# VectorE's clamp and shift of the decoded weights, walked in two interleaved halves

## The chip, the cores and the metric

The kernel runs on one core of one Trainium2 chip. The metric is the device time of one execution in microseconds. Three runs of the kernel before took 690.2, 690.53 and 690.93 us, median 690.53 us. All times below are microseconds unless marked ns, counted from the start of the profiled execution's span.

## The reference

Two stages. First an attention for 8 batches of 8 heads, 576 positions and 64 columns a head, through 32 packed queries p: the packed queries attend to k and v, and q attends to the packed result. Then a feed-forward layer on its output, 4608 tokens of 512 columns, hidden width 2048:

```python
def sm_attn(qq, kk, vv):
    s = scale * np.matmul(qq, kk.transpose(0, 1, 3, 2))
    s = s - np.max(s, axis=-1, keepdims=True)
    a = np.exp(s)
    a = a / (np.sum(a, axis=-1, keepdims=True) + 1e-09)
    return np.matmul(a, vv)
p_packed = sm_attn(p, k, v)
out = sm_attn(q, p_packed, p_packed)
...
h = x @ w_in
g = 0.5 * h * (1.0 + erf(h * inv_sqrt2))
return (g @ w_out).astype(np.float32)
```

The weights `w_in` (512 x 2048) and `w_out` (2048 x 512) reach the kernel as float64, 8 bytes an element, that is as two 32-bit words each.

## The kernel before

The work is cut into 16 units: four pairs of batches by four blocks of 512 hidden columns. For each unit TensorE multiplies the packed attention result with its block of `w_in` ("wps", L1582), the second attention's weights with that ("h", L1662 for the first unit, L1671 for the others), ScalarE applies the gelu (L1703), and TensorE multiplies the result with `w_out` ("o", L1733 to L1735, later L1922). The first matrices are split into a high and a low part (VectorE, L1712 for the gelu's result, L1300 and L1598 for others), so that three fast products make one precise one.

The weights are decoded once, in 32 tiles of 128 partitions by 512 elements, within the first 190 us: 8 tiles for each of the four blocks of hidden columns. The decode of one tile (`decode`, from L1427) goes over three engines. A DMA brings the raw words (L1441 or L1445). ScalarE puts the absolute high word into the tile's first half `t` (L1453) and the scaled low word into `full` (L1455; for two tiles of the first block GpSimd does that, L1460). VectorE then works on `t` in three instructions: a clamp of the high word between two limits (L1467), a shift left by three bits with a mask (L1468), both in place and with one tensor as source, and the return of the sign bits from the raw words (L1474), with two tensors as sources. GpSimd adds `full` (L1494 or L1509). For `w_out` there follow the split into two parts (ScalarE L1499, GpSimd L1516) and the differences of blocks (GpSimd L1533) that later units use.

`t` is one half of a slot of a large buffer, `memory`: 512 words of 4 bytes that lie one behind the other in each partition.

The order of every engine's instructions is written out by hand as lists of numbers (`TURNS`), replayed once when the program is built; a cost given to an operation there (0.85 for L1467 and L1468 together) decides nothing but the order in which the engines' streams are written. Each engine takes its instructions strictly in that order and waits by semaphores for the others. Until the first output product TensorE is kept busy by matmuls on zeros (L1640) at places that a table, `WARM`, names.

Two things around the decode matter for the prediction. PSUM has a ring of two buffers, `wide`, which wps and h tiles take in turn; a tile takes its buffer when the copy or the gelu that reads the tile before it in that buffer is over. And in the first unit VectorE does, in its written order between decode steps: the copies of two of the four wps tiles (L1593), transposes (L1220, L1289), maxima and sums of the softmaxes (L1238, L1278 to L1280).

Of the kernel before, what the change touches and what calls it, by code (L numbers as in the profile page):

```python
# [10 lines left out]
F32 = mybir.dt.float32  # L11
# [4 lines left out]
ALU = mybir.AluOpType  # L16
# [23 lines left out]
W_LEAST = 2.0 ** -15  # L40
W_MOST = 122880 - 2.0 ** -7
# [583 lines left out]
def packed_attention_gelu_ffn(ctx: ExitStack, tc: tile.TileContext, q, k, v, p, w_in, w_out, out):  # L625
# [12 lines left out]
    nc = tc.nc  # L638
# [44 lines left out]
    def plan(order):  # L683
# [743 lines left out]
        def decode(u, i, part, load_step, step):  # L1427
            n, f = f"{u}_{i}_{part}", u % NF
# [35 lines left out]
            t, full = both[:, 0], both[:, 1]  # L1464

            def rebias():
                nc.vector.tensor_scalar(t.bitcast(F32), t.bitcast(F32), W_LEAST, W_MOST, ALU.max, ALU.min)  # L1467
                nc.vector.tensor_scalar(t, t, 3, 0x3FFFFFF8, ALU.logical_shift_left, ALU.bitwise_and)  # L1468

            def high_word():  # L1470
                yield Op(DVE, 0.85, step, rebias, port=True, hold=holds[1])
                yield Op(
                    DVE, 0.685, step,
                    lambda: nc.vector.scalar_tensor_tensor(t, high, -0x40000000, t, ALU.bitwise_and, ALU.bitwise_or),  # L1474
                    port=True)
# [753 lines left out]
```

## Time and profile before

| | |
|---|---|
| median of 3 runs | 690.53 us (690.2 to 690.93) |
| the profiled execution | 690.13 us, span 688.3 us |
| granted TensorE clock, mean | 0.998 |
| PE busy | 676.2 us, 98% |
| VectorE busy | 517.7 us, 75% |
| ScalarE busy | 384.2 us, 56% |
| GpSimd busy | 317.4 us, 46% |
| chain that ended last | PE 94%, DMA 3%, ACT 1%, DVE 1% |

The span runs from the first to the last instruction; the execution's own time is 1.8 us longer. PE is TensorE's matmuls, PEld its weight loads, DVE VectorE, ACT ScalarE, POOL GpSimd. A busy PE includes the matmuls on zeros. Shares over the whole span hide that the decode is a matter of the first 190 us alone, so the stretches are looked at one by one. A line of the profile such as L1467 is a line of the kernel.

### The profile page before, as it was taken

To read this page: it belongs to the slowest core of one execution; us is meant where nothing else is said; L and a number is where in the kernel's file an instruction comes from. 1 tells how busy PE (TensorE), PEld (TensorE's weight loads), DVE (VectorE), ACT (ScalarE), POOL (GpSimd) and SP (SyncE) were. 2 spreads that over 40 slices of the span, in tenths; PEclk is the share of its full clock that TensorE was granted. 3 is DMA by queue.
4 is the path that set the end of the run, shared out by engine and by line. 5 is a ranking of instruction groups with operands and counts; after the bars stand their busy time and mean duration, and the time that the engine had idled before them with its cause. 6 is when DMAs were issued, how large, how long until landed. Compare 5 with 4: busy or idle time off the path is not lost.

```text
span 688.3 us, 13110 instructions
## 1 busy us (share of the span) xinstructions
PE 676.2 (98%) x5098; PEld 555.8 (81%) x5098; DVE 517.7 (75%) x719; ACT 384.2 (56%) x602; POOL 317.4 (46%) x298
## 2 busy tenths in 40 slices
PE   8899999999999999999999999999999999999997
PEld 6668787897878897788888897877978898879885
DVE  5898988787887736788888856687888845655785
ACT  5888777766655764464565464464546455443331
POOL 4686784484460835052246733232232653333462
PEclk9999999999999999999999999999999999999999
DMA  9987999988619799999333599999616474543354
GB/s 329 337 197 211 226 253 236 288 301 224 246 55 339 225 216 219 209 214 305 106 118 132 180 232 191 197 238 236 238 62 211 113 243 147 190 123 113 133 183 138
DMA packets 183101, 140.32 MB, mean 204 GB/s; under 512 B 144128, under 2 KB 153856, under 8 KB 183040
## 3 DMA queue, kind: packets, MB, share of 16 engines
q1 hardware_dynamic: 181168, 138.44, 72.3%
q10 hardware_dynamic: 1872, 1.05, 0.6%
q8 instruction: 40, 0.66, 0.4%
q14 instruction: 21, 0.17, 0.1%
HBM read 109.05 MB, written 30.41 MB: 203 GB/s over the span
## 4 chain that ended last, share of the span: by engine, by line
PE 94%; DMA 3%; ACT 1%; DVE 1%; issue 0%; SPq 0%; ACTq 0%
PE o L1922 34%; PE h L1671 27%; PE o L1733 6%; PE o L1735 6%; PE o L1734 6%; PE wps L1582 4%; PE h L1662 2%; DMA wraws<-in_moe_w_out_dram 2%; PE s L982 2%; PE pp L1173 1%; DMA memory<-in_k_dram 1%; PE e1Tm L1086 1%; PE o_edge L1735 1%; PE o_edge L1734 1%; PE o_edge L1733 1%; PE o L1640 0%
## 5 line engine op out<-in xcount | busy, mean ns | idle before, releaser
L1922 PE MATMUL o<-rounded 128*128 128x512 f32 (+1 forms) x1014 | 249.9, 392 | 0.7 <-DVE memory L1967 0.4
L1922 PEld LDWEIGHTS o<-rounded 128*128 128x128 f32 x1014 | 183.9, 188 | 46.7 <-issue 9.1
L1671 PE MATMUL h<-a2T,wp 128*128 128x288 f32 x1440 | 207.1, 295 | 0.7 <-ACT memory L1703 0.7
L1671 PEld LDWEIGHTS h<-a2T,wp 128*128 128x128 f32 x1440 | 200.6, 188 | 8.0 <-ACT memory L1703 1.0
L1783 POOL TENSOR_TENSOR memory<-memory 128x1024 f32<-128x1024 f32 x36 | 89.3, 2482 | 126.9 <-DVE rounded L1873 61.4
L1873 DVE TENSOR_TENSOR rounded<-memory,rounded 128x1024 fp32r<-128x1024 f32 x82 | 109.8, 1345 | 36.5 <-ACT rounded L1867 33.4
L1867 ACT CAST rounded<-memory 128x1024 fp32r<-128x1024 f32 x84 | 88.0, 1052 | 87.8 <-PE o L1922 54.4
L1967 DVE TENSOR_TENSOR memory<-o,memory 128x512 f32<-128x512 f32 x124 | 82.1, 680 | 40.5 <-PE o L1922 40.3
L1696 ACT ACTIVATE memory<-h 128x576 f32<-128x576 f32 x96 | 61.6, 651 | 81.8 <-PE h L1671 78.7
L1796 POOL TENSOR_TENSOR memory<-memory 128x1024 f32<-128x1024 f32 x12 | 30.3, 2526 | 109.0 <-ACT memory L1696 109.0
L1733 PE MATMUL o<-rounded 128*128 128x512 f32 x176 | 71.2, 405 | 0.0
L1735 PE MATMUL o<-rounded 128*128 128x512 f32 x176 | 68.8, 391 | 0.0
L1734 PE MATMUL o<-rounded 128*128 128x512 f32 x176 | 68.7, 390 | 0.0
L1598 DVE TENSOR_TENSOR wp<-wps,wp 128x1024 fp32r<-128x1024 f32 x30 | 36.2, 1219 | 22.8 <-ACT wp L1593 22.7
L1733 PEld LDWEIGHTS o<-rounded 128*128 128x128 f32 x176 | 33.1, 188 | 12.5 <-issue 6.1
L891 DVE STREAM_TRANSPOSE memory<-memory 128x1152 f32<-128x1152 f32 x24 | 32.6, 1367 | 10.9 <-DMA memory<-in_k_dram 8.0
L1509 POOL TENSOR_TENSOR memory<-memory 128x512 int32<-128x512 int32 x16 | 23.5, 1471 | 34.6 <-DVE memory L1474 26.0
L1735 PEld LDWEIGHTS o<-rounded 128*128 128x128 f32 x176 | 33.0, 188 | 7.2
L1734 PEld LDWEIGHTS o<-rounded 128*128 128x128 f32 x176 | 33.1, 188 | 5.2
L1593 ACT CAST wp<-wps 128x1024 fp32r<-128x1024 f32 x30 | 29.7, 1016 | 12.9 <-PE wps L1582 12.9
L1703 ACT ACTIVATE memory<-h 128x576 f32<-128x576 f32 x32 | 20.6, 650 | 23.3 <-PE h L1671 13.8
L1582 PE MATMUL wps<-memory,pp 64*32 64x512 f32 (+1 forms) x544 | 32.8, 571 | 0.0
(160 smaller groups left out, 880.9 us busy)
## 6 DMA issues: line engine op xcount, KB each, us to landing
rounded<-ws SPq DMA_DIRECT2D x48, 512.0 KB, 4.7
rounded<-wx_s SPq DMA_DIRECT2D x36, 512.0 KB, 4.4
memory<-ws SPq DMA_DIRECT2D x24, 512.0 KB, 5.6
wraws<-in_moe_w_out_dram SPq DMA_DIRECT2D x16, 512.0 KB, 5.6
ws<-rounded SPq DMA_DIRECT2D x16, 512.0 KB, 6.1
memory<-in_v_dram SPq DMA_DIRECT2D x15, 512.0 KB, 7.3
memory<-in_k_dram SPq DMA_DIRECT2D x48, 144.0 KB, 6.0
memory<-in_q_dram SPq DMA_DIRECT2D x48, 144.0 KB, 5.2
```

The lines of the kernel that those rows point to most:

```text
L1582: nc.tensor.matmul(t[r0:r0 + 32, hh, :m], lhsT=pp[b][rows, hh, r0:r0 + 32], rhs=wi[u, hh][rows, g, cols], start=True, stop=True)
L1598: yield Op(DVE, 1.22, step, lambda: nc.vector.tensor_tensor(lo, x, hi.bitcast(F32), ALU.subtract))
L1671: nc.tensor.matmul(t[:, half, :HALF], lhsT=w[:, wpart, ch, fc], rhs=a2T[b, ch][:, apart, half * HALF:(half + 1) * HALF], start=ch == 0 and ...
L1696: lambda: nc.scalar.activation(x[:, c % 2].rearrange("p (a n) -> p a n", a=2), t[:, :, :HALF], AF.Gelu), table="gelu")
L1733: nc.tensor.matmul(t, lhsT=g[0], rhs=w[:, 0], start=first, stop=False)
L1734: nc.tensor.matmul(t, lhsT=g[0], rhs=w[:, 1], start=False, stop=False)
L1735: nc.tensor.matmul(t, lhsT=g[1], rhs=w[:, 0], start=False, stop=last)
L1783: return Op(POOL, 2.4, 0, lambda: nc.gpsimd.tensor_tensor(of(x), of(y), of(z), op))
L1867: o = op[u, m] = yield Op(ACT, 1.04, 0, lambda o: nc.scalar.copy(o[:, 0], x), [(ops, f"op_{u}_{m}")])
L1873: engine, cost, 0, lambda: on(engine).tensor_tensor(o[:, 1], x, o[:, 0].bitcast(F32), ALU.subtract), port=True)
L1922: nc.tensor.matmul(t[:, cols], lhsT=x[:, wpart], rhs=o[:, part, q, cols], start=first and q == 0 and wpart == 0 and part == 0, stop=q == 1 ...
L1967: yield Op(DVE, 0.685, 0, lambda: nc.vector.tensor_tensor(to(), x, to(), ALU.add))
```

## The change

`t`, 512 words in a row per partition, is looked at as two halves of 256 words, and the two VectorE instructions walk it with the halves as the inner dimension: word 0, word 256, word 1, word 257, and so on. 256 words of 4 bytes are 1 KB. Both instructions read and write the same words as before, in place, with the same limits, shift and mask; only the order of the words within one instruction differs. In the built program their access goes from one dimension of 512 steps of 1 word to 256 steps of 1 word outside and 2 steps of 256 words inside. L1474, which follows, still walks straight on. No instruction, wait or place in an engine's order changes; the lines below L1466 move down by one.

```diff
             def rebias():
-                nc.vector.tensor_scalar(t.bitcast(F32), t.bitcast(F32), W_LEAST, W_MOST, ALU.max, ALU.min)
-                nc.vector.tensor_scalar(t, t, 3, 0x3FFFFFF8, ALU.logical_shift_left, ALU.bitwise_and)
+                x = t.rearrange("p (a n) -> p n a", a=2)
+                nc.vector.tensor_scalar(x.bitcast(F32), x.bitcast(F32), W_LEAST, W_MOST, ALU.max, ALU.min)
+                nc.vector.tensor_scalar(x, x, 3, 0x3FFFFFF8, ALU.logical_shift_left, ALU.bitwise_and)
```

## Rows read from the trace of the kernel before

**Rows 1.** Busy time by stretch: its bounds, its length, each engine's, clock, DMA.

```profile
0.00:20.00 20.00, 16.23 (x137) 12.32 (x138) 11.54 (x24) 11.23 (x21) 8.22 (x15) 1.00 0.93 339
20.00:60.00 40.00, 38.00 (x484) 26.50 (x483) 37.90 (x72) 34.37 (x68) 31.08 (x27) 1.00 0.85 241
60.00:190.00 130.00, 129.26 (x984) 106.42 (x983) 108.06 (x160) 91.45 (x165) 77.45 (x90) 1.00 0.89 251
190.00:688.30 498.30, 492.70 (x3498) 410.51 (x3497) 360.21 (x466) 247.20 (x350) 200.60 (x166) 1.00 0.68 183
```

**Rows 2.** TensorE's waits, 45 to 200 us: in total, times, longest.

```profile
PE h L1671 <- ACT memory L1703: 0.7, 1, 0.7
```

**Rows 3.** TensorE's waits, 0 to 45 us.

```profile
PE o L1640 <- issue: 1.4, 1, 1.4
```

**Rows 4.** VectorE's timeline, 20 to 52 us: start, duration, line; in brackets idle time before.

```profile
20.79 0.43 DVE L1467 TENSOR_SCALAR memory<-memory 128x512 f32<-128x512 f32 x1 [0.73 <-ACT memory L1453]
21.26 0.71 DVE L1468 TENSOR_SCALAR memory<-memory 128x512 int32<-128x512 int32 x1
...
23.58 0.93 DVE L1467 TENSOR_SCALAR memory<-memory 128x512 f32<-128x512 f32 x1
24.55 0.43 DVE L1468 TENSOR_SCALAR memory<-memory 128x512 int32<-128x512 int32 x1
...
29.64 0.38 DVE L1467 TENSOR_SCALAR memory<-memory 128x512 f32<-128x512 f32 x1
30.06 0.43 DVE L1468 TENSOR_SCALAR memory<-memory 128x512 int32<-128x512 int32 x1
...
33.33 0.70 DVE L1467 TENSOR_SCALAR memory<-memory 128x512 f32<-128x512 f32 x1
34.07 1.26 DVE L1468 TENSOR_SCALAR memory<-memory 128x512 int32<-128x512 int32 x1
...
39.74 0.78 DVE L1289 STREAM_TRANSPOSE memory<-memory 128x576 f32<-128x576 f32 x1 [0.17 <-POOL memory L1283]
40.44 0.79 DVE L1467 TENSOR_SCALAR memory<-memory 128x512 f32<-128x512 f32 x1
41.27 1.38 DVE L1468 TENSOR_SCALAR memory<-memory 128x512 int32<-128x512 int32 x1
...
47.30 1.38 DVE L1467 TENSOR_SCALAR memory<-memory 128x512 f32<-128x512 f32 x1
48.71 0.43 DVE L1468 TENSOR_SCALAR memory<-memory 128x512 int32<-128x512 int32 x1
49.05 0.68 DVE L1593 COPY wp<-wps 128x512 f32<-128x512 f32 x1
```

**Rows 5.** Weight loads of the tile h, 48 to 53 us: ns min/median/max, first and last start.

```profile
L1662 PEld LDWEIGHTS h<-memory,wp x16: 188/190/190, 48.6 to 52.2; 128*128 128x128 f32 x16
```

**Rows 6.** The two changed lines in the whole span, columns as in rows 5.

```profile
L1467 DVE TENSOR_SCALAR memory<-memory x32: 364/430/1376, 7.5 to 188.4; 128x512 f32<-128x512 f32 x32
L1468 DVE TENSOR_SCALAR memory<-memory x32: 426/427/1405, 7.9 to 188.8; 128x512 int32<-128x512 int32 x32
```

**Rows 7.** VectorE's groups by shape, 0 to 200 us: busy us, mean ns, idle before.

```profile
L2127 DVE TENSOR_TENSOR memory<-o,memory 128x512 f32<-128x512 f32 x16 | 10.7, 684 | 3.1 <-PE o L1735 3.1
L1598 DVE TENSOR_TENSOR wp<-wps,wp 128x1024 fp32r<-128x1024 f32 x6 | 7.1, 1218 | 0.3 <-ACT wp L1593 0.2
L1474 DVE SCALAR_TENSOR_TENSOR memory<-wraw,memory 128x512 int32<-128x512 int32 x4 | 2.8, 693 | 0.1
```

**Rows 8.** ScalarE's groups by shape, 0 to 200 us.

```profile
L1059 ACT ACTIVATE memory<-memory,mx 128x576 f32<-128x576 f32 x4 | 3.1, 768 | 0.0
L1059 ACT ACTIVATE memory<-s,mx 128x576 f32<-128x576 f32 x4 | 3.0, 758 | 1.3 <-DVE mx L1051 1.1
```

**Rows 9.** GpSimd's groups by shape, 0 to 200 us.

```profile
L1460 POOL TENSOR_SCALAR memory<-wraw 128x512 int32<-128x512 uint32 x1 | 1.6, 1594 | 0.1
```

**Rows 10.** GpSimd's timeline, 46 to 49 us.

```profile
46.78 1.61 POOL L1263 TENSOR_TENSOR memory<-memory,mx 128x576 f32<-128x576 f32 x1
```

## The prediction

> **What bounds the kernel now.** I read the busy time by stretch first. In each of the three stretches from 20 us on TensorE is busy for at least 95% of the time [rows 1]; from 60 us to the end its idle time is 0.74 + 5.6 us, so what comes late there is little. The granted clock is 1.00 in every stretch. VectorE has the decode in the first 190 us alone: it is busy 37.9 of the 40 us from 20 to 60 us, and only 108.1 of the 130 us after that [rows 1]. TensorE's list of waits agrees. Between 45 and 200 us there is a single wait of 0.7 us, for ScalarE [rows 2]. Before 45 us one of the two longest is 1.4 us of "issue", in which the profile shows nothing that TensorE waited for [rows 3]; most of the others there are for loads. So the end is set by the sum of TensorE's work from about 50 us on, plus the time at which the start-up lets it begin; a change on VectorE costs time only where it makes TensorE stop.
>
> The place where that can be is read in VectorE's timeline from 20 to 52 us [rows 4]. It starts with a wait of 0.73 us for ScalarE (20.79), and from then on VectorE runs nearly back to back: the only wait of any size is 0.17 us for GpSimd (39.74). The run ends, for TensorE, in the copy of wps at 49.05 us (L1593), over at 49.73. That copy frees the PSUM buffer wps_0_1_0, which is one of the two in the ring `wide`; the ring is taken in turn by wps_0_1_0, h_2, h_3, so h_3 needs it. The 16 weight loads of h_2 and h_3 begin between 48.6 and 52.2 us [rows 5]; the ninth, h_3's first, is thus at 48.6 + 8 x 3.6 / 15 = 50.5 us. TensorE has 0.8 us to spare there, of which I count 0.76 and leave the rest for the semaphore.
>
> **The change part by part.** No instruction is added, removed or moved: the two TENSOR_SCALARs of each of 32 decoded tiles keep their 512 elements, their place and their waits. Only their walk differs: columns 0, 256, 1, 257 and so on, read and written. So there is one unknown, the new duration, and one sum.
>
> The duration today: median 430 and 427 ns [rows 6]. An operation of VectorE with two sources takes 693 ns for the same 512 elements (L1474); from 684 ns for 512 elements (L2127) to 1218 ns for 1024 (L1598) it is 534 ns for 512 more, so 1.04 ns each and about 0.15 us fixed [rows 7]. The clamp's 0.43 us less 0.15 is 0.55 ns an element: it handles two at a time. No row shows VectorE walking with a jump at every element, so the cost is bounded from both sides. The low end is nothing: L1474 reads every second word of the raw weights and is no slower than L2127; and ScalarE's exponential takes 758 ns where it reads PSUM in steps of 32 words (L1059, source s), against 768 ns where it reads SBUF straight on [rows 7, 8]. Below nothing I see one way only, the second rival. The high end is the slowest row for these 512 elements on any engine, GpSimd's 1594 ns in L1460 [rows 9], 1.16 us more per instruction. I take 0.69 us, the row of L1474, because it is VectorE's own on the same tile and it is what comes out if the jump takes away the second element of a turn or, equally, if each pair takes two turns (0.15 + 2 x 0.28 = 0.71). So +0.26 us per instruction.
>
> [...]
>
> The sum. Eight instructions lie before 20 us (a count of the timeline), where VectorE is busy 11.5 of 20 us [rows 1] and the run of rows 4 opens with a wait for ScalarE, whose weights a DMA brings; their 8 x 0.26 us fit into such waits, and I count nothing. If that cover were gone, they could add 2.1 us at most. From 20.79 to 48.71 us there are twelve [rows 4]: 12 x 0.26 = 3.12 us, one behind the other, since VectorE has no idle time between them. GpSimd's work in this stretch waits for VectorE and shifts with it, so it hides nothing: the run of L1263 at 46.78 us [rows 10], behind which the clamp at 47.30 takes 1.38 us, is fed by VectorE itself. Less 0.17 us (the wait at 39.74) and less 0.76 us (h_3's room) that is 2.19 us by which h_3 starts later. TensorE has no idle time from there to 179 us to win it back.
>
> After 50 us: the other 44 of the 64 instructions (32 of each line [rows 6], less 8 and 12), the last at 188.8 us, 44 x 0.26 = 11.4 us against 130 - 108.1 = 21.9 us of idle VectorE from 60 to 190 us [rows 1]. TensorE waits for no VectorE result in this stretch [rows 2], so I count nothing; the cover is the idle time, and it is gone at 21.9 / 44 = 0.50 us per instruction at the latest, earlier where the idle time lies in the wrong places. So the profiled execution of 690.13 us (span 688.3, 1.8 outside it) would become 692.3 us; the median of 690.53 us becomes **692.7 us**.
>
> **The rivals.** (A) *The jump is free*, or something on the way to the chip straightens the walk, so that the change does not do what it says: 0.43 us stays, and the time is 690.5 us. For it speak the rows of L1059 and L1474 named above; against it, that neither is a jump on VectorE. [...]
>
> (B) *VectorE drops to one element per turn and thereby stops shutting out GpSimd*, the case that is not slower. The clamps now take up to 1.38 us when they meet GpSimd's work [rows 4, 10], so they wait for one another. With 0.69 us each and no such wait, the twelve of rows 4 take 8.3 us, where they now take 9.25: the run ends 0.95 us earlier. TensorE takes little of it, as h_3 has room already; the most is the 0.7 us wait at 179 us [rows 2]: 689.8 to 690.5 us. Against it: the median of either line is 0.43 us [rows 6], so at least half of these instructions meet nobody, and those get slower. It decides only if the two-element mode is lost. [...]
>
> (C) *The jump costs both*: one element per turn and two turns for each, 0.15 + 2 x 0.53 = 1.2 us, +0.79 us per instruction. Then VectorE itself is the bound: 56 instructions from 20 to 190 us add 44 us against 2.1 + 21.9 = 24 us of idle time, so +20 us at least, and up to 64 x 0.79 = 51; I put it at +27, 717 us. It begins where the idle time no longer suffices: at +0.4 us per instruction I expect +5 to +9 us, since TensorE's waits start before all idle time is used.
>
> **How the numbers follow.** What a measurement of this kernel can tell from no change is about 0.2%, 1.4 us. The forecast, a price of 0.12 to 0.35 us per instruction, has 0.55: 12 x 0.12 - 0.93 = +0.5 us at its low end (691.0) and 12 x 0.35 - 0.93 = +3.3 us at its high end, with another 1 us because the later stretch begins to lose (694.8). Within it, below 0.19 us per instruction, the sum stays under 1.4 us; I give that 0.14. A has 0.24, B 0.05 and C with its first part 0.16. Slower by over 0.2% is 0.41 + 0.16 = 0.57; within 0.2% is 0.14 + 0.24 + 0.02 = 0.40; faster 0.03, the best of B and chance. The range goes from 690.0 us, which holds A, to 700 us, which takes in C's first part; left out are the heavy end of C and the best of B. The likeliest case alone is 691.0 to 694.8 us.
>
> **What would show it.** Rows of L1467 and L1468 with a median near 690 ns, and some still over 1 us beside GpSimd, confirm the price and the mode; a maximum no longer above 0.75 us means B, a median of 430 means A. The copy of wps at 49.05 us should be about 3 us later and h_3's weight load about 2.2 us later, with a wait of TensorE for VectorE there; from 60 to 190 us TensorE should show no new wait for VectorE, and VectorE's busy time from 20 to 60 us should fill the stretch. The prediction is wrong if the duration lies outside 0.55 to 0.78 us, if h_3 starts on time although it is 0.69, or if new waits of TensorE turn up after 60 us.

## The result, and the profile after

The changed kernel takes 697.65 us (median of four runs, 697.08 to 698.24) beside 690.73 us for the kernel before in the same job: ratio 1.0102, 95% interval [1.0084, 1.0121], so 7.0 us slower. (Such ratios here and below compare runs at the usual granted clock; one run further down had an execution of 953 us at a mean clock of 0.655, which its ratio leaves out.) The forecast was 692.7 us in a range of 690.0 to 700 us: the direction and the range hold, but the likeliest case, 691.0 to 694.8 us, does not hold the time. It was +2.2 us and became +7.0 us. The profiled execution of after took 697.08 us (span 695.3), 6.95 us more than that of before.

The page's chain of work that ended last was PE 94%, DVE 1% before; now it is PE 83%, DVE 10%. VectorE has come onto the path. Where, the busy time by stretch tells (bounds, length, then PE, PEld, DVE, ACT, POOL, each with its instructions, clock, DMA):

```profile
0.00:20.00 20.00, 15.50 (x134) 11.28 (x135) 14.11 (x24) 11.33 (x21) 7.21 (x14) 1.00 0.93 341
20.00:60.00 40.00, 36.36 (x475) 24.40 (x474) 38.11 (x67) 31.86 (x63) 30.11 (x24) 1.00 0.83 237
60.00:190.00 130.00, 126.80 (x954) 101.70 (x954) 124.76 (x158) 87.92 (x161) 82.91 (x88) 1.00 0.88 239
```

Against [rows 1] VectorE's busy time rises by 2.6 us in the first stretch and by 16.7 us from 60 to 190 us, where its idle time falls from 21.9 to 5.2 us. TensorE, which had 0.74 us idle there, now has 3.2. The granted clock is 1.00 everywhere, as before.

TensorE's waits from 45 to 200 us (in total, times, longest), where [rows 2] has one row:

```profile
PE o L1736 <- DVE rounded L1713: 1.8, 1, 1.8
PE h L1672 <- ACT memory L1704: 0.7, 1, 0.7
PE e1Tm L1086 <- ACT memory L1704: 0.3, 1, 0.3
PE h L1663 <- DVE wp L1594: 0.3, 1, 0.3
PE h L1672 <- DVE pT L958: 0.2, 1, 0.2
```

Four of the five were not there, three of them for VectorE, and the longest is for L1713, the split of the gelu's result, which was not a changed line at all. Comparing the start of the same matmul in both traces, TensorE is 2.64 us late at h_3 (the place of [rows 5], 50.78 us before), 3.0 at 64, 3.8 at 90, 5.9 at 104 and 6.9 by 200 us; from there the delay stays. So some 2.6 us come from the start-up and 4.3 us from the stretch behind it. Most of the 2.6 us is there long before h_3: TensorE is on time until 26.7 us, then stops at a matmul on zeros and is 2.0 us late behind it. In its waits before 45 us this is now the longest row; L909 is a copy of transposed inputs out of PSUM.

```profile
PE o L1641 <- DVE memory L909: 1.9, 1, 1.9
```

The two changed instructions in the whole span, against [rows 6] (ns min/median/max, first and last start):

```profile
L1468 DVE TENSOR_SCALAR memory<-memory x32: 626/787/1829, 7.3 to 195.2; 128x512 f32<-128x512 f32 x32
```

```profile
L1469 DVE TENSOR_SCALAR memory<-memory x32: 657/730/1778, 8.0 to 195.9; 128x512 int32<-128x512 int32 x32
```

The three instructions of VectorE's part of the decode by shape, 0 to 200 us (busy us, mean ns, idle before), first of before, then of after:

```profile
L1474 DVE SCALAR_TENSOR_TENSOR memory<-wraws,memory 128x512 int32<-128x512 int32 x28 | 20.9, 749 | 0.5
L1468 DVE TENSOR_SCALAR memory<-memory 128x512 int32<-128x512 int32 x32 | 20.0, 624 | 1.1
L1467 DVE TENSOR_SCALAR memory<-memory 128x512 f32<-128x512 f32 x32 | 19.3, 602 | 7.5 <-ACT memory L1453 7.4
```

```profile
L1468 DVE TENSOR_SCALAR memory<-memory 128x512 f32<-128x512 f32 x32 | 31.1, 971 | 1.4 <-ACT memory L1453 1.2
L1469 DVE TENSOR_SCALAR memory<-memory 128x512 int32<-128x512 int32 x32 | 28.3, 884 | 1.1
...
L1475 DVE SCALAR_TENSOR_TENSOR memory<-wraws,memory 128x512 int32<-128x512 int32 x28 | 25.1, 898 | 0.5
```

The mean of the clamp goes from 602 to 971 ns and that of the shift from 624 to 884 ns, 0.31 us more on average. L1475 became slower too, although nothing was done to it: 749 to 898 ns.

VectorE's timeline at the two ends of the stretch of [rows 4], and at the copy that TensorE waits for:

```profile
21.15 0.88 DVE L1468 TENSOR_SCALAR memory<-memory 128x512 f32<-128x512 f32 x1 [0.76 <-ACT memory L1453]
...
26.51 1.48 DVE L1475 SCALAR_TENSOR_TENSOR memory<-wraws,memory 128x512 int32<-128x512 int32 x1
...
28.17 0.54 DVE L909 COPY memory<-o 128x384 f32<-128x384 f32 x1
...
52.69 0.67 DVE L1594 COPY wp<-wps 128x512 f32<-128x512 f32 x1
```

The first row stood at 20.79 us before, so the first eight instructions left only 0.36 us behind. The sign return in the second row took 0.69 us (25.01) and the copy L909 stood at 25.88: it is 2.29 us late. The copy of wps in the last row stood at 49.05: it is 3.64 us late.

### The profile page after: what moved, and what is told of

It is laid out like the page before. It is cut to its first block, busy times and chain, and to the rows that moved or that the text cites. A ratio compares the mean times of both kernels' runs of the same rounds, so it can differ in the third digit from the quotient of the medians.

```text
span 695.3 us, 13110 instructions
## 1 busy us (share of the span) xinstructions
PE 678.1 (98%) x5098; PEld 554.4 (80%) x5098; DVE 542.0 (78%) x719; ACT 384.4 (55%) x602; POOL 324.5 (47%) x298
## 4 chain that ended last, share of the span: by engine, by line
PE 83%; DVE 10%; DMA 3%; issue 1%; SPq 1%; ACT 0%; POOL 0%; DVEq 0%; ACTq 0%; POOLq 0%
PE o L1923 34%; PE h L1672 26%; PE o L1734 5%; PE o L1736 5%; PE o L1735 5%; PE wps L1583 4%; DVE memory L1468 2%; PE s L982 2%; DMA wraws<-in_moe_w_out_dram 1%; DVE memory L1475 1%; DVE rounded L1713 1%; DVE memory L1469 1%; PE pp L1173 1%; DMA memory<-in_k_dram 1%; PE e1Tm L1086 1%
```

## The experiments

Two questions were open: what the price per instruction consists of, and by which way 7 us come of it. The first group of runs asks both: one walks pairs of words, two interleave only a part of the tiles, and one keeps the straight walk but makes VectorE's decode longer. The edits are against the changed kernel.

**Pairs of adjacent words.** Words 0, 1, 256, 257, and so on.

```diff
-                x = t.rearrange("p (a n) -> p n a", a=2)
+                x = t.rearrange("p (a n two) -> p n a two", a=2, two=2)
```

> The two halves are interleaved by pairs of adjacent words (0, 1, 256, 257, 2, 3, ...) instead of word by word, so the 1 KB jumps stay but half as many. Theory J (the price is that every element of a walk lies apart from the one before): both instructions go back to 0.43 us and the kernel to the time of before, 690.5 us (within 1 us). Rival D (any second dimension in the walk, or any 1 KB jump, costs): 0.55 to 0.70 us each, and the kernel at +3 to +7 us.

690.66 us, ratio 1.0003 [0.9993, 1.0013]; the clamp is back at nearly the old price:

```profile
L1468 DVE TENSOR_SCALAR memory<-memory x32: 376/468/1539, 7.5 to 187.6; 128x512 f32<-128x512 f32 x32
```

So a walk between the two halves costs next to nothing as such (38 ns in the median, nothing in the time), and it is not one more dimension that costs; the jump at every single word does.

**Only the first block of hidden columns** (the 8 tiles decoded in the start-up), and **only the other three** (24 tiles):

```diff
+                x = t.rearrange("p (a n) -> p n a", a=2) if u == 0 else t
```

```diff
+                x = t.rearrange("p (a n) -> p n a", a=2) if u > 0 else t
```

> The interleaved walk in the first block of hidden columns alone: 8 of the 32 tiles, 16 instructions, all but four of those before 49 us. If the start-up loss (2.6 us on TensorE at 50.8 us in the changed kernel) comes from VectorE's own run there, 12 - 4 = 8 instructions of that run keep their price: 8 x 0.27 - 0.93 = +1.2 us, up to +2 with GpSimd's collisions, and nothing after 60 us. Rival S (the later loss is only a consequence of the late start, with orders that no longer fit): +2.6 us and a further +4 after 60 us, +6 to +7 in all.

> The interleaved walk in the other 24 tiles alone, 48 instructions, four of them before 50 us. If the later loss is its own (44 longer instructions against VectorE's idle time): TensorE loses 3 to 4.5 us between 60 and 160 us, and the kernel is at +3.5 to +5 us. By rival S, which puts the later loss down to the late start: under +1.5 us.

The first block alone: 693.73 us, 1.0053 [1.0037, 1.0068]. Its delay of TensorE is 2.4 us at h_3 and 2.9 at the end. It lost more than the +1.2 to +2 us expected, and by another gate: its list of waits from 45 to 200 us has no row for VectorE, but TensorE stopped for 1.99 us at 28.70 us, again for the copy L909, and was 2.3 us late ahead of h_3 already. The others alone: 694.11 us, 1.0061 [1.0044, 1.0079]; TensorE 0.4 us late at 51, 0.8 at 64, 1.6 at 90, 3.5 at 99, 4.0 at 224 us, with this wait in the list of 45 to 200 us:

```profile
PE o L1736 <- DVE rounded L1713: 1.9, 2, 1.7
```

The two losses, 3.45 and 3.83 us, add to 7.3 us where the whole has 7.0: neither part hides behind the other, and rival S, by which the later loss follows from the late start, is out: the later 24 tiles, for which I had counted nothing in the prediction, cost 3.83 us by themselves.

**A longer decode without a jump.** The straight walk, and behind each of the two instructions two small writes of 48 words to a buffer that nobody reads:

```diff
-                x = t.rearrange("p (a n) -> p n a", a=2)
+                x = t
+                nc.vector.memset(pad, 0.0)
+                nc.vector.memset(pad, 0.0)
```

> The straight walk, with two small fills of 48 words behind each of the two instructions: VectorE is taken up for some 0.22 to 0.27 us more per instruction, as in the changed kernel, but GpSimd is not shut out in that time. Theory C (the loss after 50 us comes from the longer exclusion between VectorE and GpSimd, which stretches other instructions): +2 to +3 us, nearly all before 60 us. Rival O (occupancy alone does it, VectorE's idle time lies in the wrong places): +6 to +7.5 us as in the changed kernel. No part of the computation is left out.

689.95 us, 0.9991 [0.9979, 1.0004]. This settled nothing: the small writes, 98 ns each, overlap the large ones (the first starts at 30.29 us, where the clamp ends at 30.33; the second ends at 30.56, where the shift has begun at 30.48) and lengthen an undisturbed tile by only 0.18 us, where the interleaved walk takes 0.52 us more (1.40 in place of 0.88 us from the clamp to the return of the signs).

**The same with three small writes each.**

> Three fills of 48 words behind each of the two straight instructions, since two lengthened a tile's decode by 0.18 us alone. One more is 0.17 us each, so VectorE should be taken up for about 0.52 us more per tile, as by the interleaved walk (1.40 us from the clamp's start to the sign step's, where the kernel before has 0.88). Theory C (the loss after 60 us comes from VectorE and GpSimd shutting each other out for longer): +2 to +3.5 us in all, TensorE losing under 1 us after 60 us. Rival O (occupancy alone): +6 to +7.5 us, with 4 us lost after 60 us. No part of the computation is left out.

The timeline of one tile (L1469 is here the clamp, L1482 the return of the signs):

```profile
31.46 0.38 DVE L1469 TENSOR_SCALAR memory<-memory 128x512 f32<-128x512 f32 x1
...
32.87 0.64 DVE L1482 SCALAR_TENSOR_TENSOR memory<-wraws,memory 128x512 int32<-128x512 int32 x1
```

From the clamp to the return of the signs it is now 1.41 us, as in the changed kernel (31.69 to 33.09 us, 1.40); before it was 0.88 (29.64 to 30.52; [rows 4] has the first two instructions). The time: 696.33 us, 1.0083 [1.0069, 1.0098], and in TensorE's waits again the split, here on line 1720:

```profile
PE o L1743 <- DVE rounded L1720: 1.4, 2, 1.0
```

So a VectorE that is busy 0.5 us longer per tile, with its instructions walking straight, costs 6.1 us. But in its trace TensorE is 3.7 us late at h_3 and 6.2 by 200 us: 2.5 us were lost behind the start-up, between the under 1 us of theory C and the 4 us of rival O, and against 4.3 in the changed kernel. The rest may be that VectorE and GpSimd hold each other up for longer, as theory C has it: from 60 to 190 us GpSimd's instructions take 0.94 us on average in the changed kernel (82.91 us, 88 of them), 0.86 before (77.45, 90), and 0.87 and 0.89 with two and three small writes (79.37, 91; 78.36, 88); and all 128 small writes of the run with two took the same 98 ns. But these are one trace each, the intervals of the two ratios overlap, and I don't claim it. A reservation: the granted clock of this profile was 0.89 from 30 to 45 us, as in that of the first block alone, where the changed kernel had 1.00, so a part of the start-up delay in these two traces may be the clock's.

**Which side pays, and is the two-element mode lost?** Ten forms one behind the other on VectorE alone, four times, behind the end of the kernel with a straight decode (its time of 712.92 us says nothing). In order: straight; source interleaved; destination interleaved; both; both in place; pairs; four quarters interleaved; even words then odd words; and with two sources (a maximum) straight and interleaved:

```diff
+            nc.vector.tensor_scalar(b, one, W_LEAST, W_MOST, ALU.max, ALU.min)
+            nc.vector.tensor_scalar(b, two(one), W_LEAST, W_MOST, ALU.max, ALU.min)
+            nc.vector.tensor_scalar(two(b), one, W_LEAST, W_MOST, ALU.max, ALU.min)
+            nc.vector.tensor_scalar(two(b), two(one), W_LEAST, W_MOST, ALU.max, ALU.min)
...
```

> The kernel before with a series of instructions behind its end, on 512 words of a free stretch of the buffer, with GpSimd at rest: the clamp straight on, with an interleaved source, an interleaved destination, both, both in place, by pairs of words, over four quarters, and first all even then all odd words; then a maximum of two sources, straight and interleaved. Its whole time says nothing. Theory J (a walk without adjacent words takes two turns for each where it has one, the two-element mode stays): straight 0.43 us, both interleaved 0.67 to 0.70, pairs 0.43, four quarters 0.67 or more, even then odd about 0.67; one side alone 0.60 to 0.70; the two-source maximum 0.69 straight and 1.0 to 1.25 interleaved. Rival M (the two-element mode is lost): both interleaved 0.69, but then one side alone also 0.69 and the two-source maximum, which has no such mode, 0.69 in both walks.

```profile
690.62 0.43 DVE L2218 TENSOR_SCALAR memory<-memory 128x512 f32<-128x512 f32 x1
691.08 0.43 DVE L2219 TENSOR_SCALAR memory<-memory 128x512 f32<-128x512 f32 x1
691.55 0.62 DVE L2220 TENSOR_SCALAR memory<-memory 128x512 f32<-128x512 f32 x1
692.21 0.66 DVE L2221 TENSOR_SCALAR memory<-memory 128x512 f32<-128x512 f32 x1
692.90 0.67 DVE L2222 TENSOR_SCALAR memory<-memory 128x512 f32<-128x512 f32 x1
693.60 0.43 DVE L2223 TENSOR_SCALAR memory<-memory 128x512 f32<-128x512 f32 x1
694.06 0.72 DVE L2224 TENSOR_SCALAR memory<-memory 128x512 f32<-128x512 f32 x1
694.81 0.43 DVE L2225 TENSOR_SCALAR memory<-memory 128x512 f32<-128x512 f32 x1
695.27 0.69 DVE L2226 TENSOR_TENSOR memory<-memory 128x512 f32<-128x512 f32 x1
696.00 1.09 DVE L2227 TENSOR_TENSOR memory<-memory 128x512 f32<-128x512 f32 x1
```

Three readings. Reading with the jump is free (second row, 0.43); writing with it costs 0.19 us (third, 0.62); both cost 0.23 (fourth). With two sources, which the prediction's estimate of 1.04 ns an element puts at one element per turn, the jump takes an instruction from 0.69 to 1.09 us: that is what the two cost together. The clamp's 0.67 is far below, so it still handles two at a time, as far as a two-source operation can stand for it; with the destination alone interleaved its 0.62 is even under the 0.69 of the straight two-source row. And the even-then-odd walk steps over every second word at 0.43 us, so it is not adjacency alone that counts.

**That walk in the kernel, and four quarters.**

```diff
+                x = t.rearrange("p (n a) -> p a n", a=2)
```

```diff
+                x = t.rearrange("p (a n) -> p n a", a=4)
```

> The walk goes over all even words and then over all odd ones, a step of 8 bytes. Theory J as an account by adjacency alone: no two words follow each other, so 0.67 to 0.70 us each and the kernel at +5 to +8 us as changed. Rival N (only a far jump costs, since the sign step's source, which also steps by 8 bytes, costs nothing): 0.43 us and the time of before.

> The walk goes over four quarters in turn, a jump of 512 bytes at each word and back after four. If the price is paid for every element that is not next to the one before: 0.67 to 0.70 us as with two halves, and the kernel at +6 to +8 us. If the number of stretches that are open at once counts: clearly more than 0.70 us each, and the kernel beyond +10 us.

The clamp in the first (690.28 us, 1.0005 [0.9992, 1.0019]) and in the second (699.85 us, 1.0136 [1.0119, 1.0154]):

```profile
L1468 DVE TENSOR_SCALAR memory<-memory x32: 366/444/1379, 7.5 to 188.6; 128x512 f32<-128x512 f32 x32
```

```profile
L1468 DVE TENSOR_SCALAR memory<-memory x32: 679/824/1868, 7.7 to 198.1; 128x512 f32<-128x512 f32 x32
```

A price of 0.72 in place of 0.66 us for the undisturbed instruction makes the loss 9.6 in place of 7.0 us: at this size, where the idle time is used up, 0.06 us more on 64 instructions, 3.8 us, comes out at 2.6 us (an estimate from one difference). The time lies between the two cases expected, +6 to +8 and beyond +10 us.

**Where in the later stretch.** Only the second block (u == 1), only the third and fourth (u >= 2), and the changed kernel with the split that TensorE waits for put ahead of the decode tile before it; the same move in the kernel before as a control.

```diff
+                x = t.rearrange("p (a n) -> p n a", a=2) if u == 1 else t
```

```diff
-        "260 311 264 43 322 653 559 594
+        "260 311 653 264 43 322 559 594
```

(In these lists 264 is the decode tile, 653 the split.)

> Only the 8 tiles of the second block of hidden columns (u == 1, decoded from about 45 to 92 us) are walked interleaved, the other 24 straight. In the run where the second to fourth blocks (24 tiles) were interleaved, TensorE's delay was 0.8 us at 63.8, 1.6 at 90 and 3.5 at 99.3 us, 4.0 at 224. Theory P (place decides): nearly all of that loss comes from this block and from the tiles around 95 us, since the written order leaves VectorE no room there; this kernel loses 2 to 3.5 us, 692.5 to 694 us. Rival E (every one of the later instructions costs alike): 8 of 24 tiles, a third of 3.8 us, 1.3 us, 691.6 us.

> The other side: only the 16 tiles of the third and fourth blocks (u >= 2, decoded from about 92 to 196 us) are walked interleaved. Theory P: 0 to 1 us, 690.3 to 691.5 us, unless the two tiles decoded beside L1713 at 95 us (which are the first of this block) open a wait of TensorE by themselves; later than 105 us nothing is lost. Rival E: two thirds of 3.8 us, 2.5 us, 692.8 us, with the delay growing evenly from 92 to 196 us.

> All 32 tiles interleaved as in the changed kernel, and VectorE's split of the gelu's result (L1713) that TensorE waited for at 105 us (1.8 us, its input ready at 98.55 us) put ahead of the decode tile before it in VectorE's written order: it can then start at about 99.0 instead of 103.3 us. Theory P: this wait of TensorE goes, and the kernel gains 1.3 to 2.2 us on the changed one, 695.5 to 696.4 us, unless the decode tile that is pushed back makes a wait of the same size behind it. Rival (the late results are late everywhere, so the next one takes its place): 697 to 698 us.

> Control: the kernel before, straight walk, with the same move of one split (L1712) ahead of one decode tile. TensorE has no wait there before the change (none for VectorE from 45 to 200 us), so both theories expect no change, 690.0 to 691.0 us; a gain would make it a version that beats both.

The kernel before spread more in this job (688.8 to 692.6 us, median 691.09), so a difference of 1 us is not settled by it. The second block alone: 1.0016 [0.9996, 1.0035]; the third and fourth: 1.0017 [1.0002, 1.0032]. By the times the two can't be told apart. By one trace each they can: TensorE's delay grows by 3.3 us from 45 to 150 us with the second block, and by nothing with the other two (0.2 us by 200), where the 24 tiles together gave 4.1 us. That speaks for place against an equal price for all; but the times, +1.1 us by the ratio with at most +2.4, don't bear out the 3.3 us, and I leave the size open. The wait of 1.7 us for L1713 that the 24 tiles had is in neither of the two traces, so it takes the lateness of the second block and the first tiles of the third together. And the "nothing" of the other two has a rival: that kernel was late as a whole before they began, while the raw words come by DMA, which may have given their decode more room. In the trace of the third and fourth block another thing is seen, ahead of any interleaved tile: TensorE is 3.4 us late at 46 us. TensorE's timeline, and busy time there, columns as above:

```profile
40.01 1.65 PE L1641 MATMUL o<-still 128*128 128x256 bf16 x7 [2.66 <-issue]
```

```profile
40.00:46.00 6.00, 5.99 (x36) 4.05 (x36) 2.96 (x6) 2.73 (x4) 5.84 (x5) 0.50 0.21 82
```

TensorE stood idle for 2.66 us, where it had 1.38 in the kernel before, and from 40 to 46 us the granted clock was 0.50, where it was 1.00 before: of the 4.1 us by which it fell back from 38 to 46 us 1.3 are the longer idle time, and the rest, 2.8, I put down to the clock, an estimate by difference. The idle time alone does not decide it: in the control below TensorE stood idle for 2.47 us from 30 to 45 us (busy for 12.53 of the 15 us), here for 2.66 (12.34), and the clock stayed at 1.00. This kernel is the same as before up to there. So the start-up delay in a single trace can be the clock's, and is not to be taken for the change's without the clock beside it; that of the changed kernel (2.64 us) was read at 1.00. In the moved kernel's trace, as in the first block's, it was lower (0.91 from 30 to 45 us).

The move: 697.76 us, 1.0094 [1.0068, 1.012], against 1.0102 without it: no gain that these runs can show. The control: 690.96 us, 1.0003 [0.9988, 1.0018]. VectorE's timeline and TensorE's of the moved kernel:

```profile
99.70 1.77 DVE L1713 TENSOR_TENSOR rounded<-memory,rounded 128x512 fp32r<-128x512 f32 x1
...
108.69 0.97 DVE L1713 TENSOR_TENSOR rounded<-memory,rounded 128x512 fp32r<-128x512 f32 x1
```

```profile
109.71 0.50 PE L1736 MATMUL o<-rounded 128*128 128x512 f32 x1 [1.33 <-DVE rounded L1713]
```

The split starts at 99.70 us in place of 103.29, and TensorE no longer waits for it: its delay is 4.6 us on both sides of the place where it had risen by 1.9 (to 6.0 us soon behind). But the next split ends at 109.66 us, because the decode tile that was pushed back and the transposes stand ahead of it, and TensorE stops there for 1.33 us: the delay rises to 6.5 us. My theory that this gate costs falls, as far as one trace and four runs can tell; what costs is a VectorE that is 6 to 9 us late from 95 to 160 us in the changed kernel, and the gate is just a place where that shows.

## Why the prediction was right in direction and wrong in size

**The price per instruction** was set at +0.26 us, with "two turns for each pair" or "one element per turn" as the reason. Alone it is 0.66 to 0.43, +0.23 us; in the kernel the medians rose by 0.36 and 0.30 us, the means by 0.37 and 0.26, 0.31 on average. So the value was good for the undisturbed instruction and low for the kernel; of the medians, 787 and 730 ns, the clamp's lies just outside the 0.55 to 0.78 us that I had named as the test. Of the two reasons "one element per turn" has the rows of 0.62 and 1.09 us against it. The other, two turns for each pair (0.71 us), stays an estimate: it is near the 0.66 us of both sides together, but no run shows turns.

**Rival A, a free jump**, had rested on reads with jumps (L1059, L1474). They were evidence for reads, and reads are free (0.43 us alone); the write pays (0.62), of which no row that I had shown was an example. **Rival B**, a VectorE that no longer meets GpSimd, fell too: its sign was a maximum under 0.75 us, and the longest were 1.83 and 1.78. That one element per turn would end these waits was an assumption of mine: L1474, with two sources, took up to 1.44 us before.

**Before 20 us: nothing.** Right: VectorE is 1.94 us late behind its eighth instruction and 0.36 us at the ninth (21.15 against 20.79), since the waits for ScalarE take the rest up.

**From 20.79 to 48.71 us: 12 x 0.26 less two reserves, 2.19 us.** Nearly right in size, but the path only in part. The copy is 3.64 us late, of which 0.36 were there at 20.79, so 3.28 us in place of 3.12: the twelve instructions took 2.99 us more, 0.25 each, and the sign return at 26.51 us 0.79 more, of which 0.5 us were made good. h_3 is 2.64 us late, so it had 1.0 us of room and not 0.76; it starts when the copy is over, as forecast. But the prediction looked at h_3 alone, and TensorE had been stopped before, by a copy that it did not name: L909, at 28.76 us, behind the first four of the twelve. From there on it was about 2 us late, 2.15 ahead of h_3, and the wait for the copy of wps (0.33 us) only brought it to 2.64. Without the gate that I named, some 2 us of this loss would have been there; that the sum came so near is partly luck. The wait of 0.17 us for GpSimd gave nothing back, as GpSimd shifts with VectorE: VectorE was 3.04 us late ahead of it and 3.03 behind it.

**After 50 us: "I count nothing; the cover is the idle time".** This is the step that failed, worth 4.3 of the 7.0 us. The 11.4 us set against the idle time were too few: added up one by one, VectorE's instructions from 50 to 190 us took 20.4 us longer, 14.2 of them the 44 changed ones (0.32 each), 3.5 the sign returns and 2.7 other unchanged lines (L1552, L1712, L1300). And the idle time was no common reserve: 5.2 us of it were left over, and TensorE stopped all the same. The prediction had "earlier where the idle time lies in the wrong places"; it lay there at 0.31 us. The stretch around 95 us shows it. Before:

```profile
86.53 0.68 DVE L1712 TENSOR_TENSOR rounded<-memory,rounded 128x512 fp32r<-128x512 f32 x1
88.46 0.43 DVE L1467 TENSOR_SCALAR memory<-memory 128x512 f32<-128x512 f32 x1 [1.25 <-ACT memory L1453]
88.92 1.41 DVE L1468 TENSOR_SCALAR memory<-memory 128x512 int32<-128x512 int32 x1
...
91.42 1.35 DVE L1467 TENSOR_SCALAR memory<-memory 128x512 f32<-128x512 f32 x1 [0.37 <-ACT memory L1453]
92.81 1.39 DVE L1468 TENSOR_SCALAR memory<-memory 128x512 int32<-128x512 int32 x1
...
94.85 0.81 DVE L1712 TENSOR_TENSOR rounded<-memory,rounded 128x512 fp32r<-128x512 f32 x1
```

After:

```profile
92.99 1.77 DVE L1713 TENSOR_TENSOR rounded<-memory,rounded 128x512 fp32r<-128x512 f32 x1
94.68 1.83 DVE L1468 TENSOR_SCALAR memory<-memory 128x512 f32<-128x512 f32 x1
96.55 0.72 DVE L1469 TENSOR_SCALAR memory<-memory 128x512 int32<-128x512 int32 x1
97.30 1.80 DVE L1475 SCALAR_TENSOR_TENSOR memory<-wraws,memory 128x512 int32<-128x512 int32 x1
99.02 1.78 DVE L1468 TENSOR_SCALAR memory<-memory 128x512 f32<-128x512 f32 x1
100.84 0.71 DVE L1469 TENSOR_SCALAR memory<-memory 128x512 int32<-128x512 int32 x1
101.58 1.79 DVE L1475 SCALAR_TENSOR_TENSOR memory<-wraws,memory 128x512 int32<-128x512 int32 x1
103.29 1.75 DVE L1713 TENSOR_TENSOR rounded<-memory,rounded 128x512 fp32r<-128x512 f32 x1
```

Before, two decode tiles stand between two splits, with 1.25 and 0.37 us of waiting for ScalarE between them. After, these waits are gone: this reserve of 1.6 us was used up, though ScalarE itself was 3.5 to 3.9 us late there, and it was too small. VectorE enters with the first split 6.45 us late (86.53 to 92.99) and leaves with the last one 8.44 us late (94.85 to 103.29). The first split takes 1.1 us longer, and between the two lie the six instructions of two decode tiles. Before, three of the six took 1.35 to 1.41 us; after, four take 1.78 to 1.83, beside long work of GpSimd such as

```profile
94.17 1.75 POOL L1517 TENSOR_TENSOR rounded<-memory,rounded 128x512 fp32r<-128x512 f32 x1
...
97.25 2.98 POOL L1534 TENSOR_TENSOR memory<-memory 128x512 f32<-128x512 f32 x2
```

The six are busy for 8.63 in place of 5.96 us, 2.67 us more, where four changed instructions at 0.31 us would make 1.24. So here the long ones, one more of them and each longer, cost as much again as the jump. That this is GpSimd's doing is read from the place: of the 96 decode instructions of VectorE in the changed kernel 32 take over 0.76 us, and every one of these lies beside work of GpSimd (so do 21 of the other 64, for over 0.3 us). No run has the changed walk in this stretch with GpSimd at rest. At the end stands TensorE, with no room of its own:

```profile
105.09 0.50 PE L1736 MATMUL o<-rounded 128*128 128x512 f32 x1 [1.77 <-DVE rounded L1713]
```

That TensorE waited for no VectorE result in this stretch [rows 2] was true, and told only that VectorE was in time, not by how much. The split of 94.85 us ended at 95.66, and TensorE's matmul that needs it started at 99.30: 3.6 us of room. In the changed kernel the split ends at 105.04, 9.4 us later; less 3.6 that is the 5.8 us by which this matmul is late, 3.9 of which TensorE had brought along. This room, result by result, is what I should have read in place of the sum of idle time.

**Rival C** said that at +0.4 us per instruction the later stretch begins to lose, "+5 to +9 us". Its mechanism is what happened, at 0.3 us and not at 0.4.

**The rows that would show it**: a wait of TensorE for VectorE's copy of wps came (L1663, 0.3 us), and "new waits of TensorE after 60 us" were named as what proves the forecast wrong; they turned up.

## What to carry to other kernels

Idle time of an engine in a chain of engines is not a reserve to be summed: what counts is, for each of its results that the bounding engine takes, how long that result lay ready before it was taken. This holds for every such result on the way, the first as well as the one that looks tightest. And longer instructions can make their unchanged neighbours longer too: here 6.2 of the 20.4 us. When an operation of VectorE like this clamp, 0.43 us for 128x512 words, is to jump by 1 KB at each word, look first at whether it writes that way (0.62 us here); reading that way, or jumping after a pair of adjacent words, cost nothing here (0.43 us each). And a gate that is moved out of the way gave nothing back here, where the engine behind it was late everywhere.

## What the runs showed of the hardware that was not expected

In the one-source clamp the cost of a 1 KB jump at every word lies almost wholly on the write side: 0.43 us straight and with an interleaved source, 0.62 with an interleaved destination, 0.66 with both, for 128x512 words. A step of two words between successive elements, on both sides, costs nothing (0.43 us), and four regions cost a little more than two (0.72). TensorE's granted clock was 0.50 from 40 to 46 us in one execution, behind 2.66 us in which it stood idle, and cost that execution over 2 us by the estimate above; in another execution, idle for 2.47 us from 30 to 45 us, it stayed at 1.00.
